# Halved weight conversion on VectorE, plain attention in two units, and a planner that knows a shared port

## The chip, the cores and the metric

The kernel runs on one core of a Trainium2 chip. The core has five engines with an instruction queue each: TensorE (PE, with its weight loads in a row of their own, PEld), VectorE (DVE), ScalarE (ACT), GpSimd (POOL) and SyncE (SP), which here only issues transfers. They work on SBUF, a memory of 128 partitions, and on PSUM, eight banks that TensorE writes and that VectorE and ScalarE read. The metric is the time of one execution on the device in microseconds; the profile gives, beside it, the span from the first instruction to the last.

## The reference

```python
B, H, S, D = 4, 8, 768, 64          # q, k, v: float32; n_global 8, n_local 96
scores = (q @ k.T) / sqrt(D)
rel = pos[:, None] - pos[None, :]
is_global = pos[None, :] < n_global
is_local = (rel >= 0) & (rel < n_local)
keep = is_global | is_local
dist = where(is_global & ~is_local, n_local, abs(rel))
scores = where(keep, scores - slopes[h] * dist, -1e9)   # slopes[h] = 2 ** -(h + 1)
a = exp(scores - max(scores)); a = a / (sum(a) + 1e-9)
x = (a @ v) for all heads, as [3072 tokens, 512]
out = ((x @ w_a) * (x @ w_b)) @ w_out        # w_a, w_b: [512, 1536], w_out: [1536, 512], float64
```

The attention is local: a block of 128 queries sees the first 8 keys of its batch and the 96 keys up to itself. The weights arrive as float64 words and are rounded to float32 by the kernel; the products are made with float32 accuracy.

## The kernel before, in words

The 24 blocks of 128 queries (4 batches of 6) are dealt to nine units of 3, 2, 3, 3, 3, 3, 3, 2 and 2 blocks. For each unit the eight heads' attention (`attention`, `split`, `att`) fills the tiles x0 to x3 (one for two heads, transposed), and the products (`moe`) then run over 12 chunks `f` of the hidden dimension: `proj` (L704) multiplies x by a chunk of w_a and of w_b into the banks p0 and p1, L742 multiplies the two, and `back` (L721) multiplies by the chunk of w_out into one bank acc per block. While unit u's products run, unit u + 1's attention is made.

TensorE multiplies float32 in a slow form, and float32r, a shorter format, in a fast one. So every operand of the products is split into a high part (a cast) and a low part (the value less its high part, `sub`, L317), and three matmuls take the place of one: high by high, low by high, high by low. `att` does the same with queries, keys, values and probabilities (qh, ql, kk, vv, ph). Only unit 0 (`u < PLAIN`, PLAIN = 1) has plain float32 matmuls in its attention (L537, L615). Unit 1 (`u < SLIM`) takes its values in three small matmuls (L637), the later units in one with both parts side by side (L651) and two additions (L664).

One block of one head goes through: scores into a bank psS; L553 on VectorE, which adds the distances and finds the maximum; L569, the exponential with its sum, on ScalarE; L576 and L577, two tiny VectorE instructions for the reciprocal; `norm` (L581 on ScalarE or L583 on VectorE or GpSimd); the transposes L592 into psT; the copy to ph on ScalarE or VectorE; in the split form L627 on VectorE, the low part; the values into psA; the copy to x.

`load_w` brings a chunk of the weights as three pieces of 512 columns and rounds each: L347 the transfer; L353 on ScalarE, the magnitude of the upper words; L360, L369 and L378 on VectorE, which clamp, shift and put the sign in; L387 on ScalarE, the lower words to a count of float32 units; L396 on GpSimd, the integer add of the two; the cast to whi on ScalarE or VectorE; the low part wlo on VectorE or GpSimd. The raw words stand in staging tiles, which are slots of weights that are not there yet. There are 36 pieces, all during unit 0's attention and products.

The order of each engine's instructions is written by a planner (`Schedule.order`). Each recorded operation has a due time and a cost in ns on every engine that may do it. The planner lets time run: an engine that is free takes, of the operations whose inputs are ready and whose tiles are free, the one that is due first, if it `wins` it. For an operation that several engines may do, `wins` compares when each would be done with it, with all the ready work that only that engine can do (`backlog`) ahead of it:

```python
at = {o: max(free[o], now) + BACKLOG * backlog[o] + c for o, c in op.costs.items()}
return at[e] <= min(at.values()) + 40.0
```

Of the kernel before, what the change touches and what calls it, by code (L numbers as in the profile page):

```python
# [39 lines left out]
PLAIN = 1  # L40
SLIM = 2
SPARE = 1
# [3 lines left out]
# Due times, in ns.  # L46
# [71 lines left out]
class Buf:  # L118
    """A tile that is allocated when the first instruction that uses it is emitted."""
# [16 lines left out]
class Op:  # L136
    def __init__(self, index, due, costs, emit, reads, writes, late):
        self.index, self.due, self.costs, self.emit, self.late = index, due, costs, emit, late
        self.bufs, self.after, self.before = [], [], 0
# [18 lines left out]
class Schedule:  # L158
    """Orders the recorded instructions: each engine takes, of those that are ready, the one that
    is due first. Costs are in ns; due times too, and only their order counts."""  # L160
# [12 lines left out]
    def op(self, due, emit, reads=(), writes=(), late=0.0, **costs):  # L173
        self.ops.append(Op(len(self.ops), due, costs, emit, reads, writes, late))

    def order(self):
# [5 lines left out]
        backlog = {e: 0.0 for e in self.SYNC}  # L182
        taken = set()
        out = []
        now = 0.0

        def arrive(op):
            if len(op.costs) == 1:
                backlog[next(iter(op.costs))] += sum(op.costs.values())
            for e in op.costs:  # L190
                insort(ready[e], (op.due, op.index, op))
# [17 lines left out]
        while len(out) < len(self.ops):  # L209
            started = True  # L210
            while started:
                started = False
                for e in free:
                    if free[e] > now:
                        continue
                    for item in ready[e]:
                        op = item[2]
                        if fits(op) and wins(op, e):
                            break
                    else:  # L220
                        continue
                    for o in op.costs:
                        ready[o].remove(item)
                    if len(op.costs) == 1:
                        backlog[e] -= op.costs[e]
# [5 lines left out]
                    op.engine = e  # L231
                    out.append(op)
                    free[e] = now + op.costs[e]
                    heappush(heap, (free[e], 0, op.index, op))
# [37 lines left out]
def pe(n, m=P):  # L272
    return max(n / 2.4 + 2.5, m / 1.2)


class Fast:
    def __init__(self, ctx, tc, qkv, wts, out, consts):
# [5 lines left out]
        self.used = {}  # L283
# [19 lines left out]
    def copy(self, due, out, src, n, reads, writes, psum=False):  # L303
        """out and src give access patterns when they are called."""
# [7 lines left out]
        self.plan.op(due, emit, reads, writes, act=act(n, psum), dve=dve(n, not psum))  # L312

    def sub(self, due, out, a, b, n, reads, writes):
        self.plan.op(
            due,
            lambda e: self.engine(e).tensor_sub(out(), a(), b()),  # L317
            reads,
            writes,
            dve=dve(n),  # L320
            pool=pool(n),
        )

    def load_w(self, f, due):
        """A chunk of the weights: float64 in, the float32 numbers nearest to it out, as two
        float32r parts."""
        nc, op = self.nc, self.plan.op
        tags = [(self.wp, f"w{p}{c}") for c in range(f + SPARE, NF) for p in ("hi", "lo")]
        tags += [(self.sp, f"stage{i}") for i in range(2)]
        pairs = []  # L330
# [6 lines left out]
        self.w[f] = (whi, wlo)  # L337
        for g, st in enumerate(pairs):
            raw = lambda st=st: st[:, :1024]
            words = lambda st=st: raw(st).rearrange("p (n two) -> p n two", two=2)  # L340
            low = lambda st=st: words(st)[:, :, 0]
            high = lambda st=st: words(st)[:, :, 1]
            mi = lambda st=st: st[:, 1024:]
            m = lambda st=st: mi(st).bitcast(F32)
            op(
                due,
                lambda e, g=g, raw=raw: nc.sync.dma_start(raw().bitcast(I64), self.wts[f, g]),  # L347
                writes=[(st, "lo"), (st, "hi")],
                dma=1456,
# [4 lines left out]
                [(st, "hi")],  # L354
                [(st, "m")],
                act=act(512),
# [7 lines left out]
                [(st, "m")],  # L364
                dve=dve(512, True),
# [7 lines left out]
                [(st, "m")],  # L373
                dve=dve(512, True),
# [6 lines left out]
                [(st, "hi")],  # L381
                [(st, "m")],
                dve=dve(512),
# [7 lines left out]
                [(st, "lo")],  # L391
                act=act(512),
# [3 lines left out]
                lambda e, mi=mi, low=low: self.engine(e).tensor_tensor(mi(), mi(), low(), op=ALU.add),  # L396
                [(st, "lo")],
                [(st, "m")],
                pool=pool(512),
            )  # L400
            hi = lambda g=g: whi[:, g]
            self.copy(due, hi, m, 512, [(st, "m")], [(whi, g)])
            self.sub(due, lambda g=g: wlo[:, g], m, hi, 512, [(st, "m"), (whi, g)], [(wlo, g)])

    def masks(self, due):
        """Distances of the two kinds of windows, negated, with -BIG where a key isn't kept. The
        wide window is G first keys and then the keys up to the last query's, the narrow one a
        batch's first block."""
# [20 lines left out]
        op(due, steps, [], [loc, glo, self.negd, self.negd0], dve=2600)  # L429

    def fetch(self, u, h, due):
        pl = PLANS[u]
        if not u:
            tag = f"w{('hi', 'lo')[h % 2]}{NF - 1 - h // 2}"
            self.used[tag] = h / H
            raw = self.plan.buf(self.wp, [P, 1536], F32, tag, f"raw{u}_{h}")
# [14 lines left out]
    def split(self, u, h, due, raw):  # L451
        """Queries, keys and values as two float32r parts each. The two parts of a key stand one
        above the other, so that one pass over them takes both."""
# [5 lines left out]
        if u < PLAIN:  # L459
# [8 lines left out]
            op(due, scale, reads, [qs], act=act(nq), dve=dve(nq, True))  # L468
# [6 lines left out]
        def scale(e):  # L475
# [5 lines left out]
        op(due, scale, reads, [qh], act=act(nq), dve=dve(nq, True))  # L481
# [6 lines left out]
            [ql],  # L488
            dve=dve(nq),
# [22 lines left out]
    def att(self, u, h, i, due, ops, x):  # L512
        """The attention of one block of queries and one head."""
# [256 lines left out]
    def run(self, raw0):  # L770
# [8 lines left out]
        for f in range(NF):  # L779
            self.load_w(f, t + f * steps[0] - WLEAD)  # L780
# [301 lines left out]
```

## Time and profile before

| | |
|---|---|
| device time, three runs | 857.6, 864.57 (median), 872.5 us |
| span of the profiled execution | 871.8 us |
| time of the profiled execution outside the span | not given |
| TensorE busy | 803.3 us (92%) |
| VectorE busy | 687.6 us (79%) |
| ScalarE busy | 438.2 us (50%) |
| GpSimd busy | 203.6 us (23%) |
| moved by transfers | 59.71 MB, mean 68 GB/s |

A row of a table of stretches gives the stretch in us from the span's start and its length, then each engine's busy time with the number of its instructions, the TensorE clock that was granted (1.00 is full), the share of the DMA engines' time and GB/s. A row of a group gives the line, the engine, the operation, output <- inputs with their shapes, xcount, then after the bar the busy time in us and the mean duration of one in ns, and after the second bar the time for which the engine stood idle just before them and what it waited for. A row of an order of time gives start and duration in us. Records of neighbours on one engine overlap a little, so the distance from start to start is what one instruction costs in a full queue. The weights' pieces are called wr, the rounded parts whi and wlo.

### The profile page before, as it was taken

What the parts mean: (1) busy time and instruction counts of PE and PEld (TensorE: products, weight loads), DVE (VectorE), ACT (ScalarE), POOL (GpSimd) and SP (SyncE); (2) the same over time, 40 slices, a digit from 0 to 9 for tenths busy, and PEclk for the clock granted to TensorE, in tenths of its full rate; (3) what the DMA queues carried; (4) which work ended last, traced back from release to release, by engine and by line L of the source; (5) the groups of instructions that cost most, each with busy time, mean ns of one, the idle gap of its engine ahead of it and who ended that gap; (6) DMA issues with size and microseconds to landing.
All of it is one profiled execution on the core that took longest, in us unless ns stands there. A gap on an engine that the chain in (4) does not pass through costs nothing.

```text
span 871.8 us, 14086 instructions
## 1 busy us (share of the span) xinstructions
PE 803.3 (92%) x4648; PEld 713.6 (82%) x4648; DVE 687.6 (79%) x2141; ACT 438.2 (50%) x1215; POOL 203.6 (23%) x209
## 2 busy tenths in 40 slices
PE   6987577778999999999999999999999999999996
PEld 3646457567988999998888898898899898999995
DVE  5579999999799788878787888878886777687422
ACT  4666557556565655444543564354454444465201
POOL 1366768655113110101111101011100111010000
PEclk9988899999999999999999999999999999999999
DMA  7544013321221211111122111111111111110000
GB/s 277 218 145 166 34 67 115 112 70 67 79 71 58 76 55 49 44 58 50 36 59 87 55 56 41 46 58 43 41 37 58 39 50 37 55 56 20 25 1 29
DMA packets 19233, 59.71 MB, mean 68 GB/s; under 512 B 2256, under 2 KB 2256, under 8 KB 19152
## 3 DMA queue, kind: packets, MB, share of 16 engines
q1 hardware_dynamic: 19152, 58.73, 19.4%
q8 instruction: 39, 0.64, 0.3%
q14 instruction: 42, 0.34, 0.1%
HBM read 52.43 MB, written 6.29 MB: 67 GB/s over the span
## 4 chain that ended last, share of the span: by engine, by line
PE 65%; DVE 28%; issue 4%; ACT 2%; DMA 0%; DVEq 0%; ACTq 0%
PE p L704 34%; PE acc L721 16%; PE pt L592 4%; PE pa L651 4%; DVE wr L360 3%; DVE ql L484 3%; DVE wr L378 3%; DVE x L664 2%; DVE ph L627 2%; PE ps L537 2%; DVE wlo L317 2%; PE pa L615 2%; DVE kk L317 2%; DVE wr L369 2%; PE ps L546 2%
## 5 line engine op out<-in xcount | busy, mean ns | idle before, releaser
L704 PE MATMUL p<-xh,whi 128*128 128x384 f32 (+1 forms) x864 | 291.5, 337 | 3.7 <-DVE as L310 1.2
L704 PE MATMUL p<-xl,whi 128*128 128x384 f32 (+1 forms) x864 | 277.7, 321 | 3.4 <-DVE xl L317 3.4
L704 PE MATMUL p<-xh,wlo 128*128 128x384 f32 (+1 forms) x864 | 278.8, 323 | 1.7 <-DVE wlo L317 1.7
L704 PEld LDWEIGHTS p<-xh,whi 128*128 128x128 f32 x864 | 165.3, 191 | 10.6 <-issue 1.5
L704 PEld LDWEIGHTS p<-xl,whi 128*128 128x128 f32 x864 | 165.8, 192 | 8.0 <-DVE xl L317 4.1
L704 PEld LDWEIGHTS p<-xh,wlo 128*128 128x128 f32 x864 | 165.0, 191 | 3.8 <-DVE wlo L317 3.3
L317 POOL TENSOR_TENSOR kk<-raw,kk 64x256 fp32r<-64x256 f32 (+1 forms) x70 | 66.2, 945 | 277.4 <-ACT kk L308 141.2
L569 ACT ACTIVATE t<-t,sm 128x256 f32<-128x256 f32 (+1 forms) x192 | 94.0, 490 | 61.5 <-DVE sm L553 59.3
L721 PE MATMUL acc<-whi,hl 128*128 128x512 f32 x288 | 115.4, 401 | 6.5 <-DVE hl L317 6.0
L721 PE MATMUL acc<-whi,hh 128*128 128x512 f32 x288 | 116.6, 405 | 0.9 <-DVE hh L310 0.9
L721 PE MATMUL acc<-wlo,hh 128*128 128x512 f32 x288 | 114.1, 396 | 0.0
L664 DVE TENSOR_TENSOR x<-pa,x 64x128 f32<-64x128 f32 x304 | 87.3, 287 | 13.7 <-ACT x L308 5.4
L742 DVE TENSOR_TENSOR as<-p,as 128x384 f32<-128x384 f32 (+1 forms) x108 | 54.9, 508 | 54.4 <-PE p L704 45.6
L553 DVE CUSTOM_DVE_ANT_0 t<-ps,rel 128x256 f32<-128x256 f32 x160 | 66.7, 417 | 33.6 <-PE ps L546 23.7
L308 ACT COPY as<-p 128x384 f32<-128x384 f32 (+1 forms) x100 | 44.3, 443 | 92.9 <-PE p L704 81.8
L592 PE MATMUL pt<-ident,t 128*128 128x128 f32 x352 | 76.2, 297 | 9.4 <-ACT t L581 6.1
L308 ACT CAST ph<-pt 128x256 fp32r<-128x256 f32 (+1 forms) x144 | 51.3, 356 | 57.7 <-PE pt L592 56.9
L627 DVE TENSOR_TENSOR ph<-pt,ph 128x256 fp32r<-128x256 f32 x168 | 67.0, 399 | 15.3 <-ACT ph L308 12.8
L308 ACT COPY x<-pa 64x128 f32<-64x128 f32 x127 | 32.7, 258 | 87.3 <-PE pa L651 66.9
L592 PEld LDWEIGHTS pt<-ident,t 128*128 128x128 f32 x352 | 46.1, 149 | 27.8 <-issue 10.3
L651 PE MATMUL pa<-ph,vv 128*128 128x256 f32 x280 | 61.4, 293 | 6.7 <-DVE x L664 3.3
L583 POOL TENSOR_SCALAR t<-t,sm 128x256 f32<-128x256 f32 (+1 forms) x43 | 24.8, 580 | 174.9 <-DVE sm L577 65.8
(85 smaller groups left out, 1335.1 us busy)
## 6 DMA issues: line engine op xcount, KB each, us to landing
wr<-wts SPq DMA_DIRECT2D x36, 512.0 KB, 7.9
raw<-qkv SPq DMA_DIRECT2D x32, 448.0 KB, 3.3
raw<-qkv SPq DMA_DIRECT2D x24, 384.0 KB, 3.0
raw<-qkv SPq DMA_DIRECT2D x16, 576.0 KB, 3.7
out<-o SPq DMA_DIRECT2D x24, 256.0 KB, 2.1
nv<-ns SPq DMA_DIRECT2D x1, 2.0 KB, 3.1
```

Of the source, the lines that this page charges most:

```text
L308: self.nc.scalar.copy(out(), src())
L317: lambda e: self.engine(e).tensor_sub(out(), a(), b()),
L360: lambda e, m=m: nc.vector.tensor_scalar(m(), m(), EMIN, EMAX, op0=ALU.max, op1=ALU.min),
L553: lambda e: nc.vector.tensor_tensor_reduce(t[:, :w], ps[:, :w], neg[:, :w], -(2.0 ** -(h + 1)), 3.0e38, ALU.add, ALU.min, sm[:, 0:1],),
L569: lambda e: nc.scalar.activation(t[:, :w], t[:, :w], AF.Exp, bias=sm[:, 0:1], scale=-1.0, accum_out=sm[:, 1:2]),
L592: nc.tensor.transpose(pt[:, c * P : c * P + P], t[:, c * P : c * P + P], self.ident)
L627: lambda e: nc.vector.tensor_sub(ph[:, :nch, 1], pv(), ph[:, :nch, 0]),
L651: nc.tensor.matmul(pa[:, : 2 * P], vv[:, slot].rearrange("p a d -> p (a d)"), ph[:, c].rearrange("p a q -> p (a q)"), start=c == 0, stop=c ...
L664: lambda e, rows=rows, cols=cols: nc.vector.tensor_add(dst(), pa[rows, cols], dst()),
L704: nc.tensor.matmul(p[:, :T], wt[:, which, c * P : c * P + P], xs[c][:, :T], start=c == 0 and n == 0, stop=c == NCC - 1 and n == 2,)
L721: nc.tensor.matmul(acc[i][:, :], hs[:, i * P : i * P + P], wt[:, 2], start=f == 0 and n == 0, stop=f == NF - 1 and n == 2,)
L742: lambda e, asb=asb, pb=pb: nc.vector.tensor_mul(asb[:, :T], pb[:, :T], asb[:, :T]),
```

## The change

A chunk of the weights comes in two halves of 768 columns instead of three pieces of 512; the host packs w_a, w_b and w_out of a chunk side by side and cuts in the middle. The raw words of a half stand in the slot in which its two parts will stand, and between them is a scratch tile wm, of which there are three. All arithmetic but the two ScalarE steps and the cast is VectorE's, the integer add and the low part too (`shared=False`). `part` finds the columns of a matmul in the halves.

Unit 1's attention has the plain form too (PLAIN = 2; the form of SLIM is gone). In the plain form the values of all blocks of a head go to one bank, and one copy per head takes them to x, where it was one per block.

The planner has a shared port: operations of VectorE and GpSimd that only touch SBUF (`port=BOTH`) don't overlap in its time. `wins` multiplies VectorE's and GpSimd's costs by 2, and counts as backlog only the ready work of that engine that is due earlier and has its tiles. Some costs are new: matmuls by 2.23 instead of 2.4 columns a ns, fixed costs of the plain matmuls, more for the exponential and for `norm` on ScalarE. The output leaves through two tiles of one block instead of one tile of three.

```diff
+WN = 3 * 512 // 2
-PLAIN = 1
-SLIM = 2
-SPARE = 1
+PLAIN = 2
+MBUFS = 3
+PRICE = {"dve": 2.0, "pool": 2.0}
...
         def wins(op, e):
-            at = {o: max(free[o], now) + BACKLOG * backlog[o] + c for o, c in op.costs.items()}
+            if len(op.costs) == 1:
+                return True
+            at = {}
+            for o, c in op.costs.items():
+                at[o] = max(free[o], now) + c * PRICE.get(o, 1.0)
+                for due, index, other in ready[o]:
+                    if (due, index) >= (op.due, op.index):
+                        break
+                    if len(other.costs) == 1 and fits(other):
+                        at[o] += BACKLOG * other.costs[o]
             return at[e] <= min(at.values()) + 40.0
...
                         op = item[2]
+                        if e in op.port and port > now:
+                            continue
                         if fits(op) and wins(op, e):
                             break
...
                     free[e] = now + op.costs[e]
+                    if e in op.port:
+                        port = free[e]
...
 def pe(n, m=P):
-    return max(n / 2.4 + 2.5, m / 1.2)
+    return max(n / 2.23 + 2.5, m / 1.2)
+BOTH = ("dve", "pool")
...
     def load_w(self, f, due):
-        for g in range(3):
-            tile_pool, tag = min(tags, key=lambda t: self.used.get(t[1], -1))
-            self.used[tag] = 3 * f + g
-            pairs.append(self.plan.buf(tile_pool, [P, 1536], I32, tag, f"wr{f}_{g}"))
-        whi = self.plan.buf(self.wp, [P, 3, 512], F32R, f"whi{f}", f"whi{f}")
-        wlo = self.plan.buf(self.wp, [P, 3, 512], F32R, f"wlo{f}", f"wlo{f}")
...
+        for g in range(2):
+            raw = self.plan.buf(self.wp, [P, 2 * WN], I32, f"w{f}_{g}", f"wr{f}_{g}")
+            w = self.plan.buf(self.wp, [P, 2 * WN], F32R, f"w{f}_{g}", f"wt{f}_{g}")
+            self.w[f, g] = w
+            st = self.sbuf([P, WN], I32, "wm", f"wm{f}_{g}", MBUFS)
...
             op(
                 due,
-                lambda e, mi=mi, low=low: self.engine(e).tensor_tensor(mi(), mi(), low(), op=ALU.add),
-                [(st, "lo")],
-                [(st, "m")],
-                pool=pool(512),
-            )
-            hi = lambda g=g: whi[:, g]
-            self.copy(due, hi, m, 512, [(st, "m")], [(whi, g)])
-            self.sub(due, lambda g=g: wlo[:, g], m, hi, 512, [(st, "m"), (whi, g)], [(wlo, g)])
+                lambda e, mi=mi, low=low: nc.vector.tensor_tensor(mi(), mi(), low(), op=ALU.add),
+                [(raw, "lo")],
+                [st],
+                port=BOTH,
+                dve=dve(WN),
+            )
+            hi, lo = (lambda w=w: w[:, :WN]), (lambda w=w: w[:, WN:])
+            self.copy(due, hi, m, WN, [st], [(w, "H")])
+            self.sub(due, lo, m, hi, WN, [st, (w, "H")], [(w, "L")], shared=False)
+
+    def part(self, f, which, c, n):
+        g, col = divmod(which * 512 + c, WN)
+        w = self.w[f, g]
+        return w, (lambda: w[:, col : col + n]), (lambda: w[:, WN + col : WN + col + n])
...
     def fetch(self, u, h, due):
-            tag = f"w{('hi', 'lo')[h % 2]}{NF - 1 - h // 2}"
+            tag = f"w{NF - 1 - h // 2}_{h % 2}"
...
     def att(self, u, h, i, due, ops, x, pa=None):
-            op(due, scores, reads + [qs_all], [ps], pe=4 * pe(w))
+            op(due, scores, reads + [qs_all], [ps], pe=540 if w > P else 270)
...
-            act=act(w) + 93,
+            act=act(w) + 200,
...
-        op(due, norm, [sm], [t], dve=130 + 0.52 * w, pool=243 + 0.836 * w, act=act(w))
+        op(due, norm, [sm], [t], port=BOTH, dve=130 + 0.52 * w, pool=243 + 0.836 * w, act=act(w) + 100)
...
-                        pa[:D, :P], raw[:, v0 : v0 + D], pf[:, c], start=c == 0, stop=c == nch - 1
+                        pa[:D, qs], raw[:, v0 : v0 + D], pf[:, c], start=c == 0, stop=c == nch - 1
...
-            op(due, values, reads + [pf], [pa], pe=4 * nch * pe(P, D))
-            self.copy(due, dst, lambda: pa[:D, :P], P, [pa], [(xc, part)], psum=True)
+            op(due, values, reads + [pf], [(pa, i)], pe=nch * 214)
             return
...
     def attention(self, u, start, end, raw0=None):
+            pa = None
+            if u < PLAIN:
+                tags = ("psA",) if u else FIRST["psA"]
+                pa = self.bank(tags[h % len(tags)], f"pa{u}_{h}")
             for i in range(pl.nb):
-                self.att(u, h, i, due + (i + 1) * step / pl.nb, ops, x)
+                self.att(u, h, i, due + (i + 1) * step / pl.nb, ops, x, pa)
+            if pa:
+                nq, xc = pl.nb * P, x[h // 2]
...
+                self.copy(due + step, dst, src, nq, [pa], [(xc, h % 2)], psum=True)
...
     def moe(self, u, start, step, x):
-        o = self.sbuf([P, 3, 512], F32, f"stage{u % 2}", f"o{u}")
         for i in range(pl.nb):
+            o = self.sbuf([P, 512], F32, "o", f"o{u}_{i}", 2)
```

More of the change, by code (lines that the diff above doesn't have):

```diff
@@ L136, with __init__ @@
 class Op:
-    def __init__(self, index, due, costs, emit, reads, writes, late):
+    def __init__(self, index, due, costs, emit, reads, writes, late, port):
         self.index, self.due, self.costs, self.emit, self.late = index, due, costs, emit, late
+        self.port = port
         self.bufs, self.after, self.before = [], [], 0
@@ L171, in buf, with op @@
         return b
-    def op(self, due, emit, reads=(), writes=(), late=0.0, **costs):
-        self.ops.append(Op(len(self.ops), due, costs, emit, reads, writes, late))
+    def op(self, due, emit, reads=(), writes=(), late=0.0, port=(), **costs):
+        self.ops.append(Op(len(self.ops), due, costs, emit, reads, writes, late, port))
     def order(self):
@@ L185, in order @@
         now = 0.0
+        port = 0.0
         def arrive(op):
-            if len(op.costs) == 1:
-                backlog[next(iter(op.costs))] += sum(op.costs.values())
             for e in op.costs:
@@ L310, in emit, with sub @@
                 self.nc.vector.tensor_copy(out(), src())
-        self.plan.op(due, emit, reads, writes, act=act(n, psum), dve=dve(n, not psum))
-    def sub(self, due, out, a, b, n, reads, writes):
+        port = () if psum else BOTH
+        self.plan.op(due, emit, reads, writes, port=port, act=act(n, psum), dve=dve(n, not psum))
+    def sub(self, due, out, a, b, n, reads, writes, shared=True):
         self.plan.op(
@@ L327, in load_w @@
         nc, op = self.nc, self.plan.op
-        tags = [(self.wp, f"w{p}{c}") for c in range(f + SPARE, NF) for p in ("hi", "lo")]
-        tags += [(self.sp, f"stage{i}") for i in range(2)]
-        pairs = []
-        for g in range(3):
-            tile_pool, tag = min(tags, key=lambda t: self.used.get(t[1], -1))
-            self.used[tag] = 3 * f + g
-            pairs.append(self.plan.buf(tile_pool, [P, 1536], I32, tag, f"wr{f}_{g}"))
-        whi = self.plan.buf(self.wp, [P, 3, 512], F32R, f"whi{f}", f"whi{f}")
-        wlo = self.plan.buf(self.wp, [P, 3, 512], F32R, f"wlo{f}", f"wlo{f}")
[L337 to L344, printed above, removed]
-            op(
-                due,
-                lambda e, g=g, raw=raw: nc.sync.dma_start(raw().bitcast(I64), self.wts[f, g]),
-                writes=[(st, "lo"), (st, "hi")],
-                dma=1456,
+        for g in range(2):
[3 more added lines that the diff above has]
+            st = self.sbuf([P, WN], I32, "wm", f"wm{f}_{g}", MBUFS)
+            words = lambda raw=raw: raw[:, :].rearrange("p (n two) -> p n two", two=2)
+            low = lambda words=words: words()[:, :, 0]
+            high = lambda words=words: words()[:, :, 1]
+            mi = lambda st=st: st[:, :]
+            m = lambda st=st: st[:, :].bitcast(F32)
+            op(
+                due,
+                lambda e, f=f, g=g, raw=raw: nc.sync.dma_start(raw[:, :].bitcast(I64), self.wts[f, g]),
+                writes=[(raw, "lo"), (raw, "hi")],
+                dma=2184,
             )
@@ L598, in att @@
         slots = pl.vslot[i]
-        pa = self.bank(place("psA", 1)[0], "pa" + n)
         if plain:
@@ L631, in att @@
         )
-        if u < SLIM:
-            terms = [(c, a, b) for c in range(nch) for a, b in ((0, 0), (0, 1), (1, 0))]
-            def values(e):
-                for m, (c, a, b) in enumerate(terms):
-                    nc.tensor.matmul(
-                        pa[:D, :P],
-                        vv[:, slots[c], a],
-                        ph[:, c, b],
-                        start=m == 0,
-                        stop=m == len(terms) - 1,
-                    )
-            op(due, values, [vv, ph], [pa], pe=len(terms) * pe(P, D))
-            self.copy(due, dst, lambda: pa[:D, :P], P, [pa], [(xc, part)], psum=True)
-            return
         def values(e):
@@ L755, in moe @@
         back(*prev, end)
-        o = self.sbuf([P, 3, 512], F32, f"stage{u % 2}", f"o{u}")
         for i in range(pl.nb):
+            o = self.sbuf([P, 512], F32, "o", f"o{u}_{i}", 2)
             self.copy(
-                end, lambda i=i: o[:, i], lambda i=i: acc[i][:, :], 512, [acc[i]], [(o, i)], psum=True
+                end,
+                lambda o=o: o[:, :],
+                lambda i=i: acc[i][:, :],
+                512,
+                [acc[i]],
+                [o],
+                psum=True,
             )
@@ L778, in run, with ahead @@
             steps.append(24 * pe(pl.nb * P) + pl.nb * 3 * pe(512) + nxt * H * 660 / NF)
+        xs = {0: x}
+        def ahead(u, t):
+            xs[u] = self.attention(u, t, t + (NF - SLACK) * steps[u - 1])
         for f in range(NF):
@@ L781, in run @@
         for u in range(len(UNITS)):
-            self.moe(u, t, steps[u], x)
+            self.moe(u, t, steps[u], xs[u])
             if u + 1 < len(UNITS):
-                x = self.attention(u + 1, t, t + (NF - SLACK) * steps[u])
+                ahead(u + 1, t)
             t += NF * steps[u]
```

95 lines of the change are left out of this document (54 added, 41 removed).

## The prediction

> **What bounds the kernel now.** I read the page for the span, then a table of stretches, then the groups of the stretch that stood out. The first line below is from the page, the others from the table of stretches, with the busy time of each engine (instructions in brackets), the granted TensorE clock, the DMA share and GB/s.
>
> ```profile
> span 871.8 us, 14086 instructions
> ```
> ```profile
> core 0: us, PE busy (x) PEld busy (x) DVE busy (x) ACT busy (x) POOL busy (x), PEclk, DMA share, GB/s
> 57.00:206.00 149.00, 109.33 (x557) 90.13 (x558) 148.24 (x273) 89.70 (x212) 103.74 (x83) 0.90 0.31 110
> 206.00:814.00 608.00, 596.71 (x3587) 548.32 (x3586) 492.99 (x1673) 307.76 (x892) 82.68 (x96) 1.00 0.15 51
> ```
>
> There are two regimes. From 206 to 814 us TensorE is busy 596.71 of 608 us. From 57 to 206 us, while the weights are converted, VectorE is busy 148.24 of 149 us and TensorE 109.33. The change acts mostly on that stage, so its price is read there. These are its VectorE groups (count, then busy us and mean ns of one).
>
> ```profile
> L360 DVE TENSOR_SCALAR wr<-wr 128x512 f32<-128x512 f32 x32 | 29.0, 918 | 0.0
> L378 DVE SCALAR_TENSOR_TENSOR wr<-wr 128x512 int32<-128x512 int32 x32 | 28.6, 898 | 0.0
> L369 DVE TENSOR_SCALAR wr<-wr 128x512 int32<-128x512 int32 x32 | 19.1, 600 | 0.0
> L317 DVE TENSOR_TENSOR wlo<-wr,whi 128x512 fp32r<-128x512 f32 x14 | 18.4, 1318 | 0.0
> L317 DVE TENSOR_TENSOR hl<-as,hh 128x384 fp32r<-128x384 f32 x9 | 10.2, 1137 | 0.0
> L627 DVE TENSOR_TENSOR ph<-pt,ph 128x256 fp32r<-128x256 f32 x17 | 7.0, 409 | 0.0
> L484 DVE SCALAR_TENSOR_TENSOR ql<-raw,qh 128x256 fp32r<-128x256 f32 x7 | 6.8, 967 | 0.0
> L317 DVE TENSOR_TENSOR kk<-raw,kk 64x256 fp32r<-64x256 f32 x7 | 6.2, 889 | 0.2
> L317 DVE TENSOR_TENSOR xl<-x,xh 128x384 fp32r<-128x384 f32 x3 | 4.8, 1614 | 0.0
> L310 DVE CAST whi<-wr 128x512 fp32r<-128x512 f32 x9 | 3.9, 430 | 0.0
> L317 DVE TENSOR_TENSOR vv<-raw,vv 128x256 fp32r<-128x256 f32 x3 | 3.1, 1038 | 0.0
> ```
>
> Those means are long. The next rows are of VectorE's order of time before that stage (start, duration), where GpSimd is less in the way.
>
> ```profile
> 47.36 0.42 DVE L360 TENSOR_SCALAR wr<-wr 128x512 f32<-128x512 f32 x1
> 47.69 0.16 DVE L577 RECIPROCAL sm<-sm 128x1 f32<-128x1 f32 x1
> 47.76 0.67 DVE L378 SCALAR_TENSOR_TENSOR wr<-wr 128x512 int32<-128x512 int32 x1
> 48.35 0.42 DVE L369 TENSOR_SCALAR wr<-wr 128x512 int32<-128x512 int32 x1
> ```
>
> From start to start the same L360 takes 0.33 us and L378 0.59; records overlap by some 0.08. L369 has the record of L360, so 0.33 too. The next two rows, of GpSimd's and of VectorE's order of time, show where the rest comes from: an L360 that starts while GpSimd works on two SBUF tiles ends just behind it, after 1.42 us in place of 0.42.
>
> ```profile
> 71.16 1.46 POOL L317 TENSOR_TENSOR wlo<-wr,whi 128x512 fp32r<-128x512 f32 x1 [0.83 <-DVE sm L576]
> ```
> ```profile
> 71.47 1.42 DVE L360 TENSOR_SCALAR wr<-wr 128x512 f32<-128x512 f32 x1
> ```
>
> L627, which reads PSUM, is not stretched (409 ns). So VectorE's saturation is partly waiting for GpSimd, and these are the groups it waits for, with the ScalarE cast beside them.
>
> ```profile
> L396 POOL TENSOR_TENSOR wr<-wr 128x512 int32<-128x512 int32 x32 | 46.2, 1447 | 18.4 <-DVE wr L378 12.0 <-DVE sm L577 1.8 <-DVE sm L576 1.6
> L317 POOL TENSOR_TENSOR wlo<-wr,whi 128x512 fp32r<-128x512 f32 x19 | 28.9, 1527 | 14.0 <-ACT whi L308 6.6 <-DVE sm L576 4.3 <-DVE whi L310 2.9
> L308 ACT CAST whi<-wr 128x512 fp32r<-128x512 f32 x24 | 14.6, 613 | 1.7 <-POOL wr L396 1.5
> L317 POOL TENSOR_TENSOR kk<-raw,kk 64x256 fp32r<-64x256 f32 x13 | 12.0, 923 | 1.5 <-ACT kk L308 0.6
> ```
>
> **Weight conversion, on VectorE.** Before, the stage holds 32 of 36 pieces: 29.0 + 28.6 + 19.1 + 18.4 + 3.9 = 99.0 us of records, less 119 overlaps of 0.07 to 0.08, about 90.5. After, each of the 24 halves has 768 columns, at 1.5 times the uncontested steps: 0.50 + 0.50 for L360 and L369, 0.89 for L378, 0.89 for the moved add and 0.89 for the low part. No row shows an int32 add on VectorE. L378 is nearest (int32, the same strided word, two inputs); its contested mean bounds the add above: 1.5 x 0.90 = 1.35, or 24 x 0.46 = 11 us more. Below L360's rate no two-input row goes, so 0.50 bounds it there, 9 us less. I take 0.89. That is 3.67 a half, 24 x 3.67 = 88 us in all, 78 for the same 32/36. The high cast goes to ScalarE, since VectorE counts double in the new choice: 24 x 0.61 x 1.5 = 22 us there, on an engine that has 59 us free. Saved: 12.5 us. Moving GpSimd's 75 us over costs VectorE nothing net, because it paid for them already by waiting.
>
> **Plain attention in unit 1, on VectorE.** Its 16 block-heads no longer need L627 (7.0), L484 (6.8), the kk (6.2) and vv (3.1) low parts: 23.1 us, less 34 overlaps, 20.5. The nine hl and three xl that stay wait less: down to the 0.59 that L378 takes for more columns, 9 x 0.55 + 3 x 1.0 = 8 us. What contention stays: GpSimd has 103.74 - 46.2 - 28.9 = 28.6 us in the stage, of which kk's 12.0 goes nearly whole with unit 1; that leaves at most 17. Some of it comes over to VectorE, at about half the time (0.59 for 512 columns against 1.5): I put 4 us. Of the rest the new order, in which GpSimd and VectorE don't overlap on SBUF, should let a few us collide: I put 3, bounds 0 and 17. Sum: 148 - 12.5 - 20.5 - 8 + 4 + 3 = 114 us; 102 if nothing collides and the add is quick, 139 with add and collisions at their upper ends.
>
> **The same on TensorE.** Its groups in the stage, and rows of its order of time at full rate:
>
> ```profile
> L704 PE MATMUL p<-xh,whi 128*128 128x384 f32 x92 | 36.1, 392 | 3.1 <-DVE as L310 1.2 <-DVE xh L310 1.0 <-DVE as L742 0.8
> L721 PE MATMUL acc<-whi,hh 128*128 128x512 f32 x33 | 14.1, 426 | 0.0
> L637 PE MATMUL pa<-ph,vv 128*64 128x128 f32 x96 | 11.4, 236 | 16.0 <-DVE ph L627 13.4 <-DVE sm L576 1.8 <-DVE ph L310 0.8
> L592 PE MATMUL pt<-ident,t 128*128 128x128 f32 x39 | 9.0, 318 | 5.4 <-ACT t L581 5.4
> L545 PE MATMUL ps<-kk,qh 128*128 128x256 f32 x18 | 5.9, 327 | 3.8 <-DVE sm L553 3.8
> ```
> ```profile
> 80.62 0.34 PE L704 MATMUL p<-xl,whi 128*128 128x384 f32 x1
> 80.79 0.34 PE L704 MATMUL p<-xh,wlo 128*128 128x384 f32 x1
> 80.97 0.40 PE L721 MATMUL acc<-whi,hh 128*128 128x512 f32 x1
> 81.20 0.39 PE L721 MATMUL acc<-whi,hl 128*128 128x512 f32 x1
> ```
>
> L704 comes three times 92, 0.175 us apart: 48 us. L721, three times 33 at 0.23: 23. L637 11.4, L592 9.0, L545 and its twin 36 x 0.12 (0.175 x 256/384): 4. About 96 us of work in 149. The plain form takes out L637 and 32 of the 36 (15 us) and puts in fp32 matmuls as unit 0 has them:
>
> ```profile
> 20.00:40.00 20.00, 20.00 (x70) 12.67 (x71) 12.02 (x58) 12.55 (x37) 5.11 (x9) 1.00 0.69 274
> ```
> ```profile
> 22.16 1.22 PE L537 MATMUL ps<-raw,qh 64*128 64x256 f32 x2
> 23.31 1.97 PE L615 MATMUL pa<-pf,raw 128*64 128x128 f32 x8
> 25.21 0.69 PE L592 MATMUL pt<-ident,t 128*128 128x128 f32 x2
> ```
> ```profile
> 304.42 0.38 PE L592 MATMUL pt<-ident,t 128*128 128x128 f32 x2
> ```
>
> A block's scores take 1.2 us (two records) and its values half of 1.97: 2.2, times 16 is 35 us. But a pair of transposes takes 0.69 us there and 0.38 in the later stage, so the whole of 20 to 40 runs at about half rate, though the column says clock 1.00. In a stage of full-rate matmuls I halve it: 17.5. TensorE then needs 96 - 15 + 17.5 = 98 us, or 116 if plain matmuls keep their slow pace: under or beside VectorE's 114.
>
> A rule of the Trainium skill (TensorE: Matmul & The Clock Gate, Part 1) says that about 3.4 us of sustained work brings the clock to full; by it the plain work costs the 98, not the 116. The trace speaks against it for fp32 work: 20 us shown without a gap, and still half rate.
>
> **The rest.** Unit 0's stage is the same matmuls; its x leaves PSUM in 8 copies instead of 24, on engines with 7 us in 20 free: nothing. In unit 1 all of a head's values stand in the one bank psA, so the next head's L615, and TensorE's queue behind it, waits for the copy of 256 columns: 8 waits below the 0.6 us of the 512-column cast, 5 us at most, on an engine with 16 us to spare in that stage; without that cover they come off the gain. Weights arrive in place, in their own slots, 16 of 24 with no wait at all; the SP queue holds the last 8 until unit 0's heads are done, and unit 1's loads behind them, but VectorE, which uses them, stands still for 0.8 us of 149 now, so no transfer was late; if that cover went, a load of some us once. After 206 us TensorE is the bound. There the new choice of engine moves copies from VectorE (493 of 608) to ScalarE (308): nothing, within plus or minus the 11 us that TensorE idles. The output tiles are two per block instead of one per unit; the third copy waits for a store, hidden behind the next unit's 12 or more L704 (2 us); uncovered, 2 us in six units.
>
> **The sum.** The stage is set by VectorE at 114 with TensorE at 98; two engines so close cost some friction, 2 us: 116. That is 33 us less: 871.8 - 33 = 839 in the profiled execution's terms. The page gives the span, not what lies around it; the three times are 857.6, 864.57 and 872.5, so this execution is like the longest and 7.2 above the median. In the median's terms: 864.57 - 33 = 832 us (-3.8%). Less than 2% (847.3 to 881.9) cannot well be told from no change.
>
> **Rivals.** (1) Nothing collides and the add is quick: VectorE at 102 us, TensorE at 98, no friction, 47 saved, 818. For it: GpSimd's two big groups are gone altogether. Against: engines in balance wait for each other. (2) TensorE becomes the bound: plain matmuls at 116 us, and the granted clock stays at 0.90, another 15: 131, 18 saved, 847. For it: the half-rate rows. Against: in the stage plain work is a fifth, between full-rate matmuls. (3) The conversion chain becomes the limit: three scratch tiles of 768 columns for everything in flight. Alone a chain lasts 0.9 (ScalarE, by the cast's row) + 0.5 + 0.5 + 0.9 + 0.9 + 0.9 (ScalarE) + 0.9 = 5.5 us and some handing over, so 3 tiles pass a half in about 2 us, faster than VectorE's 3.7; but if VectorE's and ScalarE's queues stretch it to 18 to 20 us, 21 halves last 126 to 140: 9 to 23 saved, about 849. Collisions at their upper end have the same size. (4) Slower: the fp32 work lets TensorE's clock fall to half through this stage, as it ran from 20 to 40 us. All matmuls at half: 2 x 98 = 196 in place of 149, 47 lost, 912. It decides from where half rate holds for two thirds of the stage (98 = 149 x (1 - c/2)); now 0.90 granted means a fifth. The Trainium skill's rule above would exclude it; the trace makes it unlikely, not impossible.
>
> **Chances.** Forecast 0.55, (1) 0.12, (2) 0.15, (3) 0.13, (4) 0.05. (2) and (3) lie about the 2% line, a third of them below. Faster 0.76, within 2% 0.19, slower 0.05. The range: the forecast's own is 821 to 844 (VectorE 103 to 126); with (1) it begins at 815 (some us below its 818), and with the larger part of (2) and (3) it ends at 853; some 0.18 is left out.
>
> **What would show it.** VectorE groups for 768 columns at means near 0.55 (one input) and 0.95 us (two), none near 1.5; no GpSimd group of the conversion; the stretch in which VectorE is full ending near 173 us, and first-unit matmuls with it; TensorE at about 0.85 busy there. Wrong: L360's successor still above 0.8 us (contention), VectorE idle in the stage before an add or a low part (chain or cast late), TensorE full with records of L704 at 0.52 (clock), or waits in front of L704 after 206 us.

## The result and the profile after

The changed kernel takes 828.73 us in the median (823.39 to 834.0) against 862.98 (857.6 to 872.5) for the kernel before: a ratio of 0.9624 with a 95% interval of 0.9554 to 0.9694, about 33 us less. The ratios, here and below, count only runs within 1.5% of their kernel's fastest, the medians count all. The forecast was 832 us and 33 us less. The profiled execution of the kernel before is like its longest (span 871.8 us), the profiled one of the changed kernel is its fastest (823.39 us), so the spans differ by more, 50.6 us; a later section looks at why.

From the page of the changed kernel, span and busy time of each engine:

```profile
span 821.2 us, 13536 instructions
PE 794.7 (97%) x4616; PEld 700.4 (85%) x4616; DVE 607.2 (74%) x2014; ACT 495.0 (60%) x1339; POOL 11.8 (1%) x20
```

GpSimd went from 203.6 us to 11.8, VectorE from 687.6 to 607.2, and ScalarE took on 57. Next, the same 90 us of the conversion stage in both kernels and then the rest of unit 1, from the table of stretches; first before, then after (the columns are those of the prediction's first table).

```profile
60.00:150.00 90.00, 64.77 (x319) 53.43 (x318) 89.69 (x153) 55.74 (x127) 65.63 (x51) 0.89 0.32 115
219.00:283.00 64.00, 62.19 (x431) 56.15 (x430) 56.86 (x208) 37.00 (x115) 12.88 (x15) 1.00 0.22 70
```
```profile
60.00:150.00 90.00, 87.55 (x437) 68.22 (x436) 88.28 (x183) 72.87 (x141) 0.00 (x0) 1.00 0.22 80
57.00:162.00 105.00, 101.37 (x504) 79.15 (x503) 101.03 (x210) 85.08 (x165) 1.02 (x1) 1.00 0.25 88
162.00:235.00 73.00, 71.33 (x498) 64.70 (x497) 65.01 (x251) 49.93 (x159) 2.02 (x2) 1.00 0.22 70
170.00:776.00 606.00, 598.68 (x3595) 547.94 (x3595) 458.06 (x1605) 360.90 (x1040) 9.63 (x11) 1.00 0.16 50
```

VectorE is as full as it was, but TensorE gets 87.55 us of work through in the time in which it got 64.77. Unit 0's products end at 162 us and not at 219. Some 9 us of these 57 were no gain: before, TensorE had begun unit 1's products ten microseconds ahead of unit 0's end, so what was left of unit 1 took 64 us, and after the change 73, at full use both times. Up to 11 us more are not the conversion's: the last copy into unit 0's x ended at 57 us in this execution and at 68 us in that of the kernel before (its rows stand in the section on TensorE's clock).

The conversion's groups after the change, from 57 to 170 us:

```profile
L333 DVE TENSOR_TENSOR wt<-wm,wt 128x768 fp32r<-128x768 f32 x22 | 20.6, 957 | 0.5 <-ACT wt L323 0.5
L409 DVE CUSTOM_DVE_ANT_0 wm<-wr,wm 128x1536 uint16<-128x1536 uint16 x21 | 19.3, 957 | 0.0
L390 DVE SCALAR_TENSOR_TENSOR wm<-wr,wm 128x768 int32<-128x768 int32 x21 | 19.3, 953 | 0.0
L323 ACT CAST wt<-wm 128x768 fp32r<-128x768 f32 x19 | 15.9, 836 | 5.6 <-DVE wm L409 5.3
L380 DVE TENSOR_SCALAR wm<-wm 128x768 int32<-128x768 int32 x21 | 11.1, 556 | 0.0
L370 DVE TENSOR_SCALAR wm<-wm 128x768 f32<-128x768 f32 x20 | 10.6, 556 | 0.0
L325 DVE CAST wt<-wm 128x768 fp32r<-128x768 f32 x3 | 1.7, 559 | 0.0
```

For 768 columns L370 has a mean of 556 ns; for 512 columns L360 had 918. Nothing waits for GpSimd any more. The moved add (L409) runs as an instruction over pairs of 16-bit words and costs what L390 costs. Of 22 casts, 19 went to ScalarE.

### The profile page after: what moved, and what is told of

The parts are those of the page before. It is cut to its first block, busy times and chain, and to the rows that moved or that the text cites. A ratio compares the mean times of both kernels' runs of the same rounds, so it can differ in the third digit from the quotient of the medians.

```text
span 821.2 us, 13536 instructions
## 1 busy us (share of the span) xinstructions
PE 794.7 (97%) x4616; PEld 700.4 (85%) x4616; DVE 607.2 (74%) x2014; ACT 495.0 (60%) x1339; POOL 11.8 (1%) x20
## 4 chain that ended last, share of the span: by engine, by line
PE 79%; DVE 14%; ACT 4%; issue 2%; DMA 1%; DVEq 0%; ACTq 0%
PE p L724 41%; PE acc L741 20%; PE pt L621 5%; PE pa L662 4%; PE ps L557 3%; PE pa L643 3%; DVE x L675 2%; DVE kk L333 2%; PE ps L566 2%; PE ps L565 2%; DVE ph L655 1%; DVE t L573 1%; DVE hl L333 1%; DVE ql L503 1%; ACT t L601 1%
## 5 line engine op out<-in xcount | busy, mean ns | idle before, releaser
L724 PE MATMUL p<-xh,wt 128*128 128x384 f32 (+1 forms) x1728 | 478.6, 327 | 3.0 <-ACT wt L323 0.9
L724 PEld LDWEIGHTS p<-xh,wt 128*128 128x128 f32 x1728 | 310.1, 189 | 14.2 <-issue 3.9
L724 PE MATMUL p<-xl,wt 128*128 128x384 f32 (+1 forms) x864 | 275.2, 319 | 0.6 <-DVE xl L333 0.6
L741 PE MATMUL acc<-wt,hh 128*128 128x512 f32 x576 | 215.3, 401 | 0.0
L724 PEld LDWEIGHTS p<-xl,wt 128*128 128x128 f32 x864 | 163.9, 190 | 4.2 <-DVE xl L333 0.9
L741 PEld LDWEIGHTS acc<-wt,hh 128*128 128x128 f32 x576 | 108.3, 188 | 19.1 <-issue 2.4
L589 ACT ACTIVATE t<-t,sm 128x256 f32<-128x256 f32 (+1 forms) x192 | 94.0, 490 | 48.7 <-DVE sm L573 47.1
L601 ACT ACTIVATE t<-t,sm 128x256 f32<-128x256 f32 (+1 forms) x153 | 75.1, 491 | 73.4 <-DVE sm L597 73.0
L741 PE MATMUL acc<-wt,hl 128*128 128x512 f32 x288 | 113.7, 395 | 0.0
L662 PEld LDWEIGHTS pa<-ph,vv 128*128 128x128 f32 x280 | 47.6, 188 | 19.9 <-DVE ph L655 7.3
L333 DVE TENSOR_TENSOR hl<-as,hh 128x384 fp32r<-128x384 f32 (+1 forms) x108 | 55.3, 512 | 11.5 <-ACT hh L323 10.2
```

Of the source, the lines that this page charges most:

```text
L589: lambda e: nc.scalar.activation(t[:, :w], t[:, :w], AF.Exp, bias=sm[:, 0:1], scale=-1.0, accum_out=sm[:, 1:2]),
L601: nc.scalar.mul(t[:, :w], t[:, :w], sm[:, 3:4])
L662: nc.tensor.matmul(pa[:, : 2 * P], vv[:, slot].rearrange("p a d -> p (a d)"), ph[:, c].rearrange("p a q -> p (a q)"), start=c == 0, stop=c ...
L724: nc.tensor.matmul(p[:, :T], wt(), xs[c][:, :T], start=c == 0 and n == 0, stop=c == NCC - 1 and n == 2,)
L741: nc.tensor.matmul(acc[i][:, :], hs[:, i * P : i * P + P], wt(), start=f == 0 and n == 0, stop=f == NF - 1 and n == 2,)
```

## The experiments

Times are medians; differences to the changed kernel are taken from 828.73 us. Each ratio is to the kernel before.

**The add back on GpSimd** (add_on_gpsimd).

```diff
-                lambda e, mi=mi, low=low: nc.vector.tensor_tensor(mi(), mi(), low(), op=ALU.add),
+                lambda e, mi=mi, low=low: nc.gpsimd.tensor_tensor(mi(), mi(), low(), op=ALU.add),
...
-                dve=dve(WN),
+                pool=pool(WN),
```

> The changed kernel with the integer add of a half (768 columns, 24 times) back on GpSimd; all else as changed, the planner knows of it. Theory (GpSimd's long SBUF operations hold VectorE up): by 1.45 us for 512 columns it takes 24 x 2.1 = 51 us on GpSimd, during which VectorE's SBUF operations wait, while VectorE saves 24 x 0.9 = 21; net 30 us more in the conversion stage, 850 to 860 us. Rival (VectorE is relieved by whatever leaves it): 820 to 829 us.

Measured: 855.42 us, ratio 0.9843 [0.9781, 0.9905]; 27 us are lost again by the medians, 19 by the ratios. Groups from 57 to 195 us:

```profile
L409 POOL TENSOR_TENSOR wm<-wm,wr 128x768 int32<-128x768 int32 x22 | 48.3, 2201 | 78.3 <-DVE wm L390 30.0 <-ACT x L323 13.3 <-issue 10.4
L333 DVE TENSOR_TENSOR wt<-wm,wt 128x768 fp32r<-128x768 f32 x22 | 25.0, 1135 | 1.0 <-ACT wt L323 0.8
L380 DVE TENSOR_SCALAR wm<-wm 128x768 int32<-128x768 int32 x22 | 15.2, 702 | 0.0
L370 DVE TENSOR_SCALAR wm<-wm 128x768 f32<-128x768 f32 x22 | 17.9, 821 | 2.6 <-ACT wm L363 2.6
```

VectorE has 21 us less to do and the kernel is slower. Its own instructions lengthen (556 to 821 and 702 ns), as the theory said, though not by the whole 48 us. The rest went into waiting: VectorE is idle for 17 of these 138 us, where it was idle for 4 of 105 in the changed kernel, and GpSimd stood for 30 us until L390 was done. That the planner's port rule kept the two apart in this way is argued from the code.

**Unit 1 split again** (unit1_split: PLAIN = 1, with the three small matmuls of SLIM):

```diff
-PLAIN = 2
+PLAIN = 1
+SLIM = 2
...
+        if u < SLIM:
+            terms = [(c, a, b) for c in range(nch) for a, b in ((0, 0), (0, 1), (1, 0))]
...
+            op(due, values, [vv, ph], [pa], pe=len(terms) * pe(P, D))
```

> The changed kernel with unit 1's attention in the split form again (values in three small matmuls, as before). Theory of the prediction (VectorE sets the stage, 20.5 us of its work left with the split form): VectorE gets back 14 to 20 us, TensorE loses 2 to 4: 840 to 850 us. Rival (TensorE, 97% busy in the stage of the changed kernel, sets it): 824 to 830 us.

Measured: 842.84 us, ratio 0.9781 [0.9736, 0.9827]; 14 us, as the theory had it. The stretch of its conversion:

```profile
57.00:188.00 131.00, 110.19 (x577) 92.89 (x577) 121.66 (x254) 102.63 (x216) 25.25 (x20) 0.91 0.32 124
```

VectorE has 121.66 us of work there against 101.03, and GpSimd is back with the low parts of kk.

**The old choice of engine** in the changed kernel (old_planner):

```diff
-                at[o] = max(free[o], now) + c * PRICE.get(o, 1.0)
...
+            at = {o: max(free[o], now) + BACKLOG * backlog[o] + c for o, c in op.costs.items()}
...
-                        if e in op.port and port > now:
-                            continue
```

> The changed kernel with the planner's old choice of engine: no shared port, no prices, the backlog counted as before; the new costs stay. Theory (the moved add does it, the planner little): GpSimd is used again for low parts and norms, some 10 to 17 us of it in the stage; 832 to 842 us. Rival (the planner is as much a cause as the add): above 845 us. Rival (planner does nothing): 826 to 831 us.

Measured: 876.69 us, ratio 1.0179 [1.0105, 1.0253]. With every other part of the change in place the kernel is 48 us slower than the changed one and slower than before. The theory (832 to 842 us) missed; the rival in which the planner is as much a cause as the add came true. The stretch to the end of unit 0's products, two groups and a wait of it (the wait's numbers are us in all, times, and the longest):

```profile
57.00:195.00 138.00, 117.28 (x524) 88.79 (x524) 130.99 (x264) 48.88 (x91) 33.84 (x28) 0.92 0.19 68
```
```profile
L319 DVE CAST wt<-wm 128x768 fp32r<-128x768 f32 x18 | 9.9, 549 | 0.0
L364 DVE TENSOR_SCALAR wm<-wm 128x768 f32<-128x768 f32 x20 | 13.5, 711 | 0.0
```
```profile
ACT wm L357 <- DVE wt L327: 65.4, 16, 11.4
```

VectorE does the casts that ScalarE could do, and ScalarE stands 65.4 us waiting for VectorE. By the code the reason is the backlog: it counts all ready work of an engine, and with the raw words in place the first ScalarE step of every half that has landed is ready, though no scratch tile is free for it. So ScalarE looks full while it idles. That reading is argued from the code; the wait is what the trace shows. GpSimd has 33.84 us of work there again, and VectorE's one-input records are longer (L364: 711 ns against 556), so a part of the 48 us may be the old stretching. The two parts were not separated.

**Without the port rule** (no_port), **and without the prices** (no_price).

```diff
-                        if e in op.port and port > now:
-                            continue
```
```diff
-PRICE = {"dve": 2.0, "pool": 2.0}
+PRICE = {"dve": 1.0, "pool": 1.0}
```

> The changed kernel, planner without the shared-port rule; prices and the new backlog stay. Theory (GpSimd and VectorE collide when the planner doesn't know of the port): GpSimd takes low parts and norms again, 10 us or more of collisions in the stage: 836 to 846 us. Rival (the prices alone keep GpSimd empty, its operations cost twice VectorE's): 825 to 832 us.

> The changed kernel with both prices at 1; port rule and new backlog stay. Theory (the old planner lost 48 us by putting casts and copies that ScalarE could do on VectorE): part of them goes back to VectorE, 24 casts of 0.5 us and some 50 copies of 0.35: 838 to 855 us. Rival (it was the backlog alone, which counted ScalarE's ready but blocked steps of all loaded halves): 826 to 832 us.

Measured: 829.03 us, 0.9613 [0.9551, 0.9675], and 831.23 us, 0.9627 [0.9575, 0.968]. Both theories fall and both rivals' times came: neither rule alone is worth more than the 2.5 us by which the second median differs. From 57 to 162 us without the port rule, and from 165 to 776 us without the prices:

```profile
57.00:162.00 105.00, 102.50 (x504) 80.46 (x503) 100.86 (x212) 83.35 (x163) 1.97 (x2) 0.98 0.23 81
```
```profile
165.00:776.00 611.00, 598.17 (x3598) 547.01 (x3597) 490.61 (x1732) 300.03 (x859) 66.77 (x84) 1.00 0.16 52
```

Without the rule GpSimd still has 1.97 us in the stage. Without the prices GpSimd has 67 us of work again where TensorE is the bound, and at most those 2.5 us are its cost. What remains of the planner's 48 us is the new backlog, or the three rules standing in for each other; the backlog alone was not run.

**One part alone, on the kernel before.** The add and the low part on VectorE (vector_only); the new choice of engine (planner_only); plain attention in unit 1, PLAIN = 2 (plain_only):

```diff
-                lambda e, mi=mi, low=low: self.engine(e).tensor_tensor(mi(), mi(), low(), op=ALU.add),
+                lambda e, mi=mi, low=low: nc.vector.tensor_tensor(mi(), mi(), low(), op=ALU.add),
...
-                pool=pool(512),
+                dve=dve(512),
...
+            self.sub(due, lambda g=g: wlo[:, g], m, hi, 512, [(st, "m"), (whi, g)], [(wlo, g)], shared=False)
```
```diff
+                at[o] = max(free[o], now) + c * PRICE.get(o, 1.0)
...
+                        if e in op.port and port > now:
+                            continue
```
```diff
-PLAIN = 1
+PLAIN = 2
```

> The kernel before with one thing changed: the integer add and the low part of the weights on VectorE, in pieces of 512. Theory: VectorE gets 36 x 0.6 us of adds and 21 x 0.6 of low parts, 34 us, and is freed of waiting for GpSimd, 40 to 48 us: 849 to 857 us. Rival (the stretched records were not GpSimd's doing, the work is simply added): 885 to 900 us. Rival (the port is nearly all of it): 838 us or less.

> The kernel before with the new choice of engine alone (port rule, prices, new backlog); conversion in pieces of 512 with its add on GpSimd, split attention in unit 1, old costs. Theory (planner and the moved add work together, GpSimd's 52 us of adds still hold VectorE up): 845 to 858 us. Rival (the planner is nearly all of the gain): 838 us or less. Rival (with the add on GpSimd the port rule makes both queue up): 863 us or more.

> The kernel before with plain attention in unit 1 alone (its copies to x still per block). Theory (VectorE sets the stage, 20 us leave it, all else as before): 843 to 850 us. Rival (the planner gives the room to other waiting, or plain matmuls slow TensorE): 855 to 866 us.

Measured: 849.56 us, 0.9894 [0.9825, 0.9963]; 855.58 us, 0.9907 [0.9874, 0.9941]; 859.25 us, 0.9979 [0.9936, 1.0021]. The first two theories hold, the third misses, and its rival (855 to 866 us) came. By the ratios the parts alone give 9, 8 and 2 us: 19 together, where the whole change gave 32. The conversion on GpSimd and VectorE, for vector_only (57 to 186 us) and plain_only (57 to 191 us):

```profile
L396 DVE CUSTOM_DVE_ANT_0 wr<-wr 128x1024 uint16<-128x1024 uint16 x31 | 22.6, 733 | 0.0
L360 DVE TENSOR_SCALAR wr<-wr 128x512 f32<-128x512 f32 x30 | 16.5, 567 | 0.0
L317 POOL TENSOR_TENSOR kk<-raw,kk 64x256 fp32r<-64x256 f32 x17 | 19.6, 1151 | 5.0 <-issue 3.4 <-ACT kk L308 0.6
L317 POOL TENSOR_TENSOR hl<-as,hh 128x384 fp32r<-128x384 f32 x10 | 12.4, 1236 | 16.7 <-ACT hh L308 13.1 <-DVE sm L576 3.6
```
```profile
L396 POOL TENSOR_TENSOR wr<-wr 128x512 int32<-128x512 int32 x30 | 46.2, 1548 | 32.6 <-DVE wr L378 26.5 <-DVE sm L577 3.7 <-DVE sm L576 1.2
L360 DVE TENSOR_SCALAR wr<-wr 128x512 f32<-128x512 f32 x29 | 27.1, 944 | 0.2 <-ACT wr L353 0.2
```

With the add moved alone, the old choice of engine fills GpSimd with other low parts, which hold VectorE up in turn (L360: 567 ns, where 417 is uncontested). With plain attention alone, the adds on GpSimd go on stretching VectorE's records (944 ns). In both, GpSimd's work took a part of the room. Why plain attention alone should give as little as 2 us isn't settled by these rows.

**Pieces of 512 columns** with all else as changed (pieces_512):

```diff
-        for g in range(2):
-            raw = self.plan.buf(self.wp, [P, 2 * WN], I32, f"w{f}_{g}", f"wr{f}_{g}")
+        for g in range(3):
+            tile_pool, tag = min(tags, key=lambda t: self.used.get(t[1], -1))
...
-            o = self.sbuf([P, 512], F32, "o", f"o{u}_{i}", 2)
+        o = self.sbuf([P, 3, 512], F32, f"stage{u % 2}", f"o{u}")
```

> The changed kernel with the weights in three pieces of 512 columns in staging tiles, as before, and the old output tile; add and low part on VectorE, plain attention and the new planner stay. Theory (planner, moved add and plain attention together make the gain, the halves save only the fixed cost of 12 x 5 instructions of 0.07 us, 4 us): 829 to 838 us. Rival (the loads in place, which don't wait for staging, and the halves carry what the three parts alone don't): 840 to 852 us.

Measured: 839.52 us (830.91 to 841.34), 0.968 [0.9587, 0.9774]: between the ranges of the theory and of the rival. It is 11 us more by the medians, 7 us more by the fastest and by the slowest runs of both, and 5 us by the ratios, whose intervals overlap. Its VectorE in the stage:

```profile
L379 DVE TENSOR_SCALAR wr<-wr 128x512 f32<-128x512 f32 x34 | 14.0, 417 | 0.3 <-ACT wr L372 0.3
```

Here too nothing stretches: 417 ns, the uncontested record of the prediction. So the gain needs the add off GpSimd, a planner that uses ScalarE, and less work for VectorE: without one of them 19, 48 and 14 us are lost. The halves add something between nothing and 11 us.

**TensorE's clock in unit 0's attention.** The scores of one block take one of two durations there. In TensorE's order of time of the changed kernel the switch is seen; the second fence is the kernel before, still slow at 46 us:

```profile
28.70 1.22 PE L557 MATMUL ps<-raw,qh 64*128 64x256 f32 x2
32.88 0.70 PE L557 MATMUL ps<-raw,qh 64*128 64x256 f32 x2
```
```profile
46.39 1.22 PE L537 MATMUL ps<-raw,qh 64*128 64x256 f32 x2
```

In the profiles the first full clock is granted anywhere from 17 us (vector_only) to 58 us (unit1_split). To see whether this is the scatter of the times, I put full-array work, whose result is not used, ahead of the first scores (warm_start), and in a second kernel also between the scores (warm_hold):

```diff
+    def push(self, bank, n):
+        b = self.ident.bitcast(BF16)
+        for _ in range(n):
+            self.nc.tensor.matmul(bank[:, : 2 * P], b[:, :P], b[:, : 2 * P], start=True, stop=True)
+
+    def warm(self):
+        b = self.bank("psA", "warm")
+        self.plan.op(-2e9, lambda e: self.push(b, WARM), [], [b], pe=2000)   # WARM = 24
```
```diff
             def scores(e):
+                if not u:
+                    self.push(ps, 2)
```

> The changed kernel with 24 matmuls of the identity (bfloat16, 256 columns, result unused) ahead of TensorE's first scores. In the profiles the clock is first granted in full between 17 and 58 us, and unit 0's attention ends between 47 and 63 us with it. Theory (this is the scatter of the times, and some 5 us of full-array work bring it early): 812 to 823 us, and less scatter than 11 us. Rival (the float32 matmuls behind it don't hold the clock): 826 to 834 us.

> As warm_start, and two more such matmuls in front of each of unit 0's 24 scores. Theory (float32 work alone doesn't count enough to hold the clock; full-array work between it does): 808 to 820 us, below warm_start. Rival (the clock holds anyway, or the 48 matmuls only cost 5 to 10 us): equal to warm_start or above it, up to 836 us.

Measured: 817.76 us (815.84 to 818.52), 0.9449 [0.9383, 0.9516], and 825.01 us (824.77 to 825.32), 0.9542 [0.9475, 0.9608]. TensorE's order of time of warm_start:

```profile
5.79 4.84 PE L801 MATMUL warm<-ident 128*128 128x256 bf16 x24 [5.79 <-DVE flag L1032]
13.48 1.20 PE L559 MATMUL ps<-raw,qh 64*128 64x256 f32 x6
18.61 0.70 PE L559 MATMUL ps<-raw,qh 64*128 64x256 f32 x2
19.23 0.44 PE L623 MATMUL pt<-ident,t 128*128 128x128 f32 x2
```

The clock is full from 10 to 41 us. The next rows are the last copies into unit 0's x, in warm_start, the changed kernel and the kernel before:

```profile
49.78 0.47 ACT L325 COPY x<-pa 64x384 f32<-64x384 f32 x1 [1.17 <-PE pa L645]
56.45 0.47 ACT L323 COPY x<-pa 64x384 f32<-64x384 f32 x1 [0.67 <-PE pa L643]
67.49 0.28 DVE L310 COPY x<-pa 64x128 f32<-64x128 f32 x1
```

So unit 0's attention ends at 50 us instead of 57 and 68 (the ends from 47 to 63 us in the expectation leave out the last values and their copies). The kernel is 11 us faster than the changed one by the medians, 5 us by the profiled executions (spans 816.4 and 821.2), and each of its four runs is faster than any run of the changed kernel: the fastest of all that ran. Its times scatter by 2.7 us instead of 10.6, but the four runs of no_price scatter by 2.2 without such matmuls; so that early full-array work shortens the kernel is shown, and that the clock makes the scatter is not. The matmuls between the scores only cost: warm_hold's clock is full from 10 us too, and it is 7 us slower than warm_start.

**The kernel before, profiled again** (before_again).

> The kernel before, a second profile. Theory (the first profile was of an execution whose clock was granted late): span 853 to 865 us, unit 0's attention ends before 60 us, and VectorE is full from there for 140 to 150 us all the same. Rival: the stage itself differs between executions, VectorE full for less than 135 us.

Measured: 873.15 us, span 871.4; again an execution with a late clock (full first at 52 us), so the expected span was missed and a second kind of execution of it was not seen. The stage was the same:

```profile
60.00:150.00 90.00, 65.06 (x318) 54.04 (x318) 89.69 (x153) 55.60 (x127) 65.85 (x50) 0.87 0.32 113
```

VectorE is full for 89.69 of 90 us, to the hundredth as in the first profile: the stage doesn't differ between these two executions.

## Why the prediction was right, point by point

**What bounds.** VectorE set the conversion stage by waiting for GpSimd: shown. Where GpSimd's adds are gone (the changed kernel, pieces_512) the one-input records are 0.556 us for 768 columns and 0.417 for 512; where they are there (add_on_gpsimd), 0.821 and 0.702 for 768.

**Weight conversion, 12.5 us.** The price of a half was right. From VectorE's order of time after the change:

```profile
72.98 0.55 DVE L370 TENSOR_SCALAR wm<-wm 128x768 f32<-128x768 f32 x1
73.44 0.15 DVE L597 RECIPROCAL sm<-sm 128x1 f32<-128x1 f32 x1
74.91 1.82 DVE L390 SCALAR_TENSOR_TENSOR wm<-wr,wm 128x768 int32<-128x768 int32 x2
76.65 1.82 DVE L409 CUSTOM_DVE_ANT_0 wm<-wr,wm 128x1536 uint16<-128x1536 uint16 x2
78.38 0.55 DVE L762 TENSOR_TENSOR as<-p,as 128x384 f32<-128x384 f32 x1
```

From start to start L370 costs 0.46, a pair of L390 1.74 and a pair of L409 1.73: 2 x 0.46 + 3 x 0.87 = 3.5 us a half against 3.67. The unknown add came out at the value taken.

**Plain attention, 20.5 us of VectorE.** As a difference of VectorE's work it is borne out (121.66 to 101.03 us with the split form and without, while GpSimd had 25.25 and 1.02); as time, it is worth 14 us on top of the other parts and 2 by itself. The sum treated it as additive, and it isn't.

**Contention.** The step of 3 us for collisions and 4 us for work coming over from GpSimd was too large: GpSimd has 1.02 us in the stage. VectorE's 114 us became 101. Of these 13 us at most 7 are the two terms; about 4 are the smaller price of a half (21 halves at 3.5 instead of 3.67), and the rest was not taken apart.

**TensorE.** 98 us were expected, 101.37 are shown busy. The plain matmuls run at full rate in the stage:

```profile
112.06 0.65 PE L643 MATMUL pa<-pf,raw 128*64 128x128 f32 x4
112.64 0.44 PE L724 MATMUL p<-xh,wt 128*128 128x384 f32 x1
113.59 0.70 PE L557 MATMUL ps<-raw,qh 64*128 64x256 f32 x2
114.21 0.50 PE L741 MATMUL acc<-wt,hh 128*128 128x512 f32 x1
```

0.58 us for values and 0.62 for scores, 1.2 for a block or 19 us in all, where 17.5 were taken. The conditions of rivals 2 and 4 are out: the granted clock in the stage is 1.00. TensorE is nevertheless as full there as VectorE (101.37 and 101.03 of 105 us); that VectorE's work still counts is seen in the split form, which is 14 us slower with VectorE busy for 121.66 and TensorE for 110.19 of 131 us. Rival 3 is out too: VectorE waits 0.5 us for a cast in the whole stage.

**The size.** Both engines are full from 60 to 150 us. From 57 us to the end of unit 0's products the stage lasted 105 us, nearer rival 1 (102 us) than the forecast (116), with 13 us less of VectorE's work than forecast. In the terms of the profiled executions the sum was too cautious by 18 us, 839 against 821.2. But that compares one of the longest executions of the kernel before with the fastest of the changed one, in which unit 0's attention ended 11 us earlier. By the ratio the kernels are 33 us apart, as forecast, and their fastest runs 34 (857.6 and 823.39). That the size was met so closely is in part luck: what the sum left on VectorE was too much, and it was worked out from a profile with a late clock. What an execution of the kernel before with an early clock looks like isn't known, since both of its profiles are late ones.

**The rest.** That the new choice of engine brings nothing was the weakest step, and the result alone doesn't show it. After the stage it holds, to 2.5 us (no_price, no_port). But in the stage the choice was taken for granted with one clause, that the high cast goes to ScalarE; in the changed kernel with the old choice, 48 us hang on it.

## What to carry to other kernels

A saturated engine whose records lengthen beside another engine's work is waiting, not working: price a move by the uncontested distance from start to start, and look who works when the record is long. Parts that relieve the same bound are not additive: alone on the kernel before they gave 9, 8 and 2 us, taken one at a time out of the changed kernel they cost 19, 48 and 14, and the whole change gave 32. The planner, which looked like a side matter, decided whether the freed time was used. Where operations are dealt out by an estimate of backlog, count only work that can start; that this rule is what made the planner's 48 us is argued here, not shown.

## What was not expected of the hardware

Float32 matmuls that fill TensorE by the record (20.00 of 20 us busy) can run at half rate for more than 40 us (until 53 us in the kernel before), and the granted-clock column shows 1.00 for that time; the durations show it (1.22 against 0.70 us for the same scores). The Trainium skill (TensorE: Matmul & The Clock Gate, Part 1) has about 3.4 us of sustained work bring the full clock. No run here shows that for the float32 work of unit 0's attention, which got it between 17 and 58 us. Full-array bfloat16 matmuls of 4.84 us were enough in the one profile of each warm kernel (full at 10 us), and the float32 work behind them then ran at full rate for 31 us in warm_start. What in the float32 work kept the clock down (its type, its half-filled array or its pauses) was not taken apart.
